# The end of a spectral mixer and MLP kernel: two-row sums, a last row tile in two pieces, and two half tiles moved

## The chip, the core and the metric

The kernel runs on one core of a Trainium2 chip. Its engines each follow an instruction stream of their own: PE multiplies matrices (PEld is its weight load), DVE, ACT and POOL work on vectors, SP issues transfers. The metric is the device time of one execution in microseconds (us), given as the median of several runs. A profile of one execution shows when every instruction ran; its span runs from the first instruction to the last.

## The reference

```
xn = layernorm(x)                       # x is 1 x 2048 x 512, float32
A  = irfft2( rfft2(xn) * (w_r + i w_i) )  # over rows and columns
h  = x @ w1 + b1  on xn:  h = xn @ w1 + b1          # w1 is 512 x 1792
B  = (h * tanh(softplus(h))) @ w2       # w2 is 1792 x 512
out = x + A + B
```

So one normalised input feeds a two-dimensional Fourier filter and a two-layer MLP with the Mish activation, and both results are added to the input.

## The kernel before

The 2048 rows are held as 16 row tiles of 128 rows, in four groups `g` of four tiles `s`. Numbers are split into two float16 halves, so a product is three passes on PE; the helper `mm3` (L68, L71, L72) issues the three.

The MLP is cut into 56 units (four groups times 14 blocks `f` of 128 hidden columns). `up(n)` makes a block of hidden values in PSUM tile `ph_g_f` (12 matmuls of 512 columns, L727); `mish` (L738, ACT), `a_hi` (L747, ACT) and `a_lo` (L750, DVE) turn it into `a_g_f`; `down(n)` multiplies it with w2 into four accumulators `pa_g_s` (12 matmuls, L68 to L72). `up` and `down` of a unit are each called a half tile. For the last row tiles of group 3, `mlp_rest` stops short of the last three blocks, and `end_of(s)` (L821 to L838) does those three for each row tile `s`, adds the result into the row tile (L837, DVE) and stores it. For `s` = 3 the columns are done in pieces with PSUM tiles `pe_0`, `pe_256`, and so on, after the rest of the accumulator was added at L816.

The Fourier branch is a stream of small units. Near its end, `dp_unit` fills PSUM tiles `psA`, which leave as `at` (L649 on ACT, L650 on DVE) and are turned through SP transfers into tiles `ai` (L656). `ip_pair` multiplies two `ai` tiles into a pair of PSUM tiles `psT` (L672); these leave as `tt` (L694 on ACT, L695 on DVE) and are stored to device memory as `d_t` (L700). When all of `d_t` is stored, it is loaded as 16 tiles `yi` (L857). The inverse along the rows makes `psY` from `yi`: for twelve of the row tiles in pairs (`s1_inverse_pair`, L108), for the four of group 0 one by one (`s1_inverse`). ACT copies `psY` into `ys` (L911, L912, or L878 for single rows), DVE makes sum and difference of a pair (L913, L914), and `add_rows` (L888 to L890) adds one row tile of `ys` into its row tile: 512 columns with the first half repeated, then 256 columns added and 256 subtracted. Row tiles of groups 0, 1 and 2 are called `m` and are stored at once (L778 for group 0, L782 otherwise); those of group 3 are called `y` and wait for the MLP.

Which half tiles stand between the steps of the Fourier stream is set by the table `HALVES`: one number for each step, saying how many half tiles are written ahead of it. From there a scheduler orders the instructions of each engine, with a few of them kept in program order; it may put a unit's matmuls inside another's. Every engine works its list strictly in order. Stores of `y` go half to SP's queue and half to ACT's. PSUM tiles tagged `f` (`psA`, `psT`, `psY`) share two buffers, and so do those tagged `h` (`ph`, `pe_0`).

Of the kernel before, what the change touches and what calls it, by code (L numbers as in the profile page):

```python
# [18 lines left out]
S, D, F = 2048, 512, 1792  # L19
P = 128  # L20
# [5 lines left out]
HALVES = (  # L26
# [4 lines left out]
)  # L31
NQ = 4
# [9 lines left out]
def spectral_mlp_kernel(ctx, tc, x, wt, w0, w1, b1, w2, cT, cIT, cM, out):  # L42
    nc = tc.nc
# [8 lines left out]
    ps_f = ctx.enter_context(tc.tile_pool(name="ps_f", bufs=2, space=PSUM))  # L52
    ps_h = ctx.enter_context(tc.tile_pool(name="ps_h", bufs=2, space=PSUM))
# [12 lines left out]
    def mm3(ps, stat, mov, start, stop, order=False):  # L66

        first = nc.tensor.matmul(ps, stat(0), mov(0), start=start, stop=False)  # L68
        if order:
            tc.keep_in_program_order(first)  # L70
        nc.tensor.matmul(ps, stat(0), mov(1), start=False, stop=False)  # L71
        nc.tensor.matmul(ps, stat(1), mov(0), start=False, stop=stop)  # L72
# [29 lines left out]
    def quarters(ps, stat, mov, order):  # L102

        for k, (hs, hm) in enumerate(PASSES):
            for r in range(2):
                for c in range(2):
                    rs, cs = slice(64 * r, 64 * r + 64), slice(64 * c, 64 * c + 64)
                    i = nc.tensor.matmul(ps(r, c)[cs], stat(r, c, hs)[rs], mov(r, c, hm)[rs], start=k == 0, stop=k == 2)  # L108
                    if order and (k, r, c) == (0, 0, 0):
                        tc.keep_in_program_order(i)  # L110
# [595 lines left out]
    macc, yacc = {}, {}  # L706
# [61 lines left out]
    def load_x(t, g, s, n):  # L768
        if g == 0:
            nc.sync.dma_start(t, xv[:, s : s + n, :])  # L770
            return
        for k in range(0, n, 2):
            for b in range(2):
                nc.sync.dma_start(t[64 * b : 64 * b + 64, k : k + 2, :], xw[:, 4 * g + s + k + b])

    def store_out(g, s, t, cs=slice(0, D)):
        if g == 0:
            nc.sync.dma_start(outv[:, s, cs], t)  # L778
            return
        for b in range(2):  # L780
            engine = nc.scalar if g == 3 and b else nc.sync
            engine.dma_start(outw[:, 4 * g + s // 2 * 2 + b, s % 2, cs], t[64 * b : 64 * b + 64])  # L782
# [13 lines left out]
    def mlp_rest(n_up, n_down, lag):  # L796

        while n_down < len(UP) - LAST:
            early = n_down % NFC == NFC - 1 and n_up - n_down == lag - 1
            if n_up < len(UP) and n_up - n_down < lag and not early:  # L800
                up(n_up)
                mish(n_up)
                a_hi(n_up)
                a_lo(n_up)
                if n_up % NFC == NFC - 1 and n_up // NFC < 3:
                    load_res(n_up // NFC)
                n_up += 1
                yield 1
            else:
                down(n_down)  # L810
                if n_down % NFC == NFC - 1:
                    mlp_end(n_down // NFC)
                n_down += 1
                yield 1
        r = yacc[3][3]
        nc.vector.scalar_tensor_tensor(r, pacc[3][3], sc["out"], r, op0=ALU.mult, op1=ALU.add)  # L816
        for s in range(4):
            end_of(s)
            yield 1

    def end_of(s):  # L821
        n = len(UP) - LAST
        g, pa, r = 3, pacc[3][s], yacc[3][s]
        for o, w in ((0, 256), (256, 128), (384, 128)) if s == 3 else ((0, D),):
            cs = slice(o, o + w)
            pool, tag = (ps_f, "f") if o == 384 else (ps_h, "h")
            ps = pool.tile([P, w], F32, tag=tag, name=f"pe_{o}") if s == 3 else pa
            for k in range(LAST):
                f = UP[n + k][1]
                mm3(  # L830
                    ps,
                    lambda i: act[n + k][:, i, s * P : (s + 1) * P],
                    lambda i: w2t[:, i, f, cs],
                    s == 3 and k == 0,
                    k == LAST - 1,
                )
            nc.vector.scalar_tensor_tensor(r[:, cs], ps, sc["out"], r[:, cs], op0=ALU.mult, op1=ALU.add)  # L837
            store_out(g, s, r[:, cs], cs)  # L838
# [24 lines left out]
    def s1_inverse(g, s):  # L863
        s2 = s
        yi = yis.pop(0)
        ps = ps_f.tile([P, 4, P], F32, tag="f", name=f"psY_{s2}")
        psr = ps.rearrange("p (b a) e -> p a b e", a=2)

        def slots(h, a):
            v = yi[:, :, h, :].rearrange("p (b a) e -> p a b e", a=2)[:, a]  # L870
            return v[:, :, ::-1] if a else v

        for a in range(2):
            mm3(psr[:, a], lambda h: sc["cIT"][:, s2, h, :], lambda h: slots(h, a), True, True, a == 0)
        if s % 2 == 0:
            ys[0] = tp.tile([P, 2, D], F32, tag="X", name=f"ys_{s2}", bufs=2)
        t = ys[0][:, s % 2]
        nc.scalar.activation(t, ps.rearrange("p a e -> p (a e)"), AF.Copy, scale=sc["k"])  # L878
        m = macc[g][:, s, :]
        add_rows(m, t)  # L880
        store_out(g, s, m)

    ys = {}

    def add_rows(m, t):
        mv = m.rearrange("p (b q) -> p b q", b=2)
        tv = t.rearrange("p (r q) -> p r q", r=2)
        nc.vector.tensor_add(mv, mv, tv[:, 0:1].to_broadcast((P, 2, 256)))  # L888
        nc.vector.tensor_add(mv[:, 0], mv[:, 0], tv[:, 1])
        nc.vector.tensor_sub(mv[:, 1], mv[:, 1], tv[:, 1])  # L890

    def s1_inverse_pair(g, s):
        s2, j = 4 * g + s, s // 2
        yi = [yis.pop(0) for _ in range(2)]
        ps = [ps_f.tile([P, 4, P], F32, tag="f", name=f"psY_{s2 + k}") for k in range(2)]
        psr = [t.rearrange("p (b a) e -> p a b e", a=2) for t in ps]

        def slots(k, h, a):
            v = yi[k][:, :, h, :].rearrange("p (b a) e -> p a b e", a=2)[:, a]
            return v[:, :, ::-1] if a else v  # L900

        for a in range(2):
            quarters(
                lambda r, c: psr[r][:, a],
                lambda r, c, h: sc["cIW"][:, s2 - 4 + c, h, :],
                lambda r, c, h: slots(c, h, a),
                a == 0,
            )
        t = tp.tile([P, 2, D], F32, tag="X", name=f"ys_{s2}", bufs=2)
        pe, po = (v.rearrange("p a e -> p (a e)") for v in ps)  # L910
        nc.scalar.activation(t[:, 0], pe, AF.Copy, scale=sc["k"])  # L911
        nc.scalar.activation(t[:, 1], po, AF.Copy, scale=sc["k"])  # L912
        nc.vector.tensor_add(t[:, 0], t[:, 0], t[:, 1])  # L913
        nc.vector.scalar_tensor_tensor(t[:, 1], t[:, 1], -2.0, t[:, 0], op0=ALU.mult, op1=ALU.add)  # L914
        if g not in macc:
            y = big.tile([P, 2, D], F32, tag="big", name=f"y_{s2}")
            load_x(y, g, s, 2)
        for h in range(2):
            m = macc[g][:, s + h, :] if g in macc else y[:, h, :]
            add_rows(m, t[:, h])  # L920
            if g in macc:
                store_out(g, s + h, m)
            else:
                yacc.setdefault(g, []).append(m)


    done = [0]
# [466 lines left out]
    for g, s, w in todo:  # L1394
        next(plan)
        (s1_inverse_pair if w == 2 else s1_inverse)(g, s)
# [136 lines left out]
```

## Time and profile before

| | us |
|---|---|
| median of 3 runs | 363.49 (363.40 to 363.56) |
| the profiled execution: its time | 363.37 |
| the profiled execution: its span | 361.6 |
| PE busy | 353.9 (98% of the span) |
| DVE busy | 278.5 (77%) |
| ACT busy | 187.7 (52%) |

The time holds about 1.8 us that the span does not. A row of the timeline reads: start, duration, engine, line, operation, output and inputs, shape, count. A duration on DVE or PE is longer than the distance to the next start, since each instruction's beginning overlaps the end of the one ahead. "SPq" and "ACTq" are the instructions of those engines that issue a transfer; the transfer itself lands later. "PEclk" or "granted clock" is the share of full speed at which PE ran; it is 0.998 over the whole span.

### The profile page before, as it was taken

To read this page: it belongs to the slowest core of one execution; us is meant where nothing else is said; L and a number is where in the kernel's file an instruction comes from. 1 tells how busy PE (TensorE), PEld (TensorE's weight loads), DVE (VectorE), ACT (ScalarE), POOL (GpSimd) and SP (SyncE) were. 2 spreads that over 40 slices of the span, in tenths; PEclk is the share of its full clock that TensorE was granted. 3 is DMA by queue.
4 is the path that set the end of the run, shared out by engine and by line. 5 is a ranking of instruction groups with operands and counts; after the bars stand their busy time and mean duration, and the time that the engine had idled before them with its cause. 6 is when DMAs were issued, how large, how long until landed. Compare 5 with 4: busy or idle time off the path is not lost.

```text
span 361.6 us, 6167 instructions
## 1 busy us (share of the span) xinstructions
PE 353.9 (98%) x2283; PEld 174.0 (48%) x2283; DVE 278.5 (77%) x543; ACT 187.7 (52%) x288; POOL 47.8 (13%) x49
## 2 busy tenths in 40 slices
PE   7999999999999999999999999999999999999994
PEld 2544444444444444545554445544554445444453
DVE  4898998886598776399998955996498933349995
ACT  5989974564654751525454365355443554445511
POOL 0020002303304500033030301130032000000000
PEclk9999999999999999999999999999999999999999
DMA  8945753699796657443611327218831524686566
GB/s 269 319 145 181 190 126 89 125 220 255 119 309 127 143 169 178 172 111 88 227 31 51 97 57 233 61 52 215 228 96 41 130 58 111 124 248 219 118 153 197
DMA packets 60702, 54.98 MB, mean 152 GB/s; under 512 B 16720, under 2 KB 49776, under 8 KB 60544
## 3 DMA queue, kind: packets, MB, share of 16 engines
q1 hardware_dynamic: 60192, 54.06, 56.6%
q10 hardware_dynamic: 480, 0.52, 0.5%
q8 instruction: 18, 0.29, 0.3%
q14 instruction: 12, 0.10, 0.1%
HBM read 34.61 MB, written 12.58 MB: 131 GB/s over the span
## 4 chain that ended last, share of the span: by engine, by line
PE 90%; DVE 6%; ACT 1%; DMA 1%; issue 0%; DVEq 0%
PE ph L727 39%; PE pa L68 13%; PE pa L71 12%; PE pa L72 12%; PE psT L672 2%; PE psS L108 1%; PE psY L108 1%; DMA x<-in_x_dram 1%; PE psA L68 1%; PE psA L71 1%; PE psA L72 1%; PE psP L516 1%; PE psP L526 1%; DVE u L425 1%; PE psP L519 1%; DVE xh L188 1%
## 5 line engine op out<-in xcount | busy, mean ns | idle before, releaser
L727 PE MATMUL ph<-xnT,w1t 128*128 128x512 f16 x672 | 153.4, 379 | 0.0
L727 PEld LDWEIGHTS <-w1t 128*128 128x128 f16 x672 | 64.6, 98 | 77.7 <-issue 2.7
L738 ACT ACTIVATE hb<-ph,b1t,fp_exp 128x512 f32<-128x512 f32 x56 | 43.2, 771 | 58.3 <-PE ph L727 58.2
L68 PE MATMUL pa<-w2t,a 128*128 128x512 f16 x181 | 68.7, 380 | 0.0
L71 PE MATMUL pa<-w2t,a 128*128 128x512 f16 x181 | 68.6, 379 | 0.0
L72 PE MATMUL pa<-w2t,a 128*128 128x512 f16 x181 | 68.6, 379 | 0.0
L750 DVE SCALAR_TENSOR_TENSOR a<-hb,ip_a,a 128x512 f16<-128x512 f32 x46 | 34.4, 749 | 34.4 <-ACT a L747 34.2
L747 ACT ACTIVATE a<-hb,ip_a 128x512 f16<-128x512 f32 x46 | 33.1, 720 | 2.3 <-DVE ip_a L288 1.2
L72 PEld LDWEIGHTS <-a 128*128 128x128 f16 x190 | 18.6, 98 | 21.0
L68 PEld LDWEIGHTS <-a 128*128 128x128 f16 x190 | 18.6, 98 | 20.8 <-issue 2.0
L71 PEld LDWEIGHTS <-a 128*128 128x128 f16 x190 | 18.6, 98 | 18.6
L249 POOL TENSOR_TENSOR xh<-xs,xh 128x512 f16<-128x512 f32 x12 | 15.4, 1292 | 56.7 <-ACT xh L223 23.4
L424 ACT ACTIVATE u<-w,sc_u 128x512 f16<-128x512 f32 x16 | 10.8, 713 | 22.1 <-DVE w L625 10.2
L531 DVE SCALAR_TENSOR_TENSOR z<-psP,z 128x512 f16<-128x512 f32 x16 | 10.8, 688 | 9.6 <-ACT z L530 9.6
L223 ACT ACTIVATE xh<-x,nb,rs 128x512 f16<-128x512 f32 x12 | 9.6, 806 | 13.1 <-DVE nb L217 11.7
L695 DVE SCALAR_TENSOR_TENSOR tt<-psT,tt 128x512 f16<-128x512 f32 x16 | 10.4, 683 | 7.3 <-ACT tt L694 7.3
L600 POOL TENSOR_TENSOR w<-X,wE 128x512 f32<-128x512 f32 x4 | 5.1, 1274 | 69.6 <-DVE X L593 69.6
L694 ACT ACTIVATE tt<-psT 128x512 f16<-128x512 f32 x16 | 8.8, 589 | 10.7 <-PE psT L672 8.8
L649 ACT ACTIVATE at<-psA 128x512 f16<-128x512 f32 x16 | 9.2, 589 | 9.4 <-PE psA L72 7.0
L156 DVE BATCH_NORM_STATS2 st<-x 128x6 f32<-128x512 f32 x16 | 10.3, 679 | 4.4 <-DMA x<-in_x_dram 4.4
L425 DVE SCALAR_TENSOR_TENSOR u<-w,sc_u,u 128x512 f16<-128x512 f32 x16 | 11.4, 747 | 2.4 <-ACT u L424 2.2
L530 ACT ACTIVATE z<-psP 128x512 f16<-128x512 f32 x16 | 9.4, 590 | 5.3 <-PE psP L526 5.2
(220 smaller groups left out, 576.7 us busy)
## 6 DMA issues: line engine op xcount, KB each, us to landing
d_y<-y SPq DMA_DIRECT2D x16, 256.0 KB, 4.2
wm<-in_wt_dram SPq DMA_DIRECT2D x8, 512.0 KB, 5.2
ai<-at SPq DMA_DIRECT2D x64, 64.0 KB, 2.2
d_t<-tt SPq DMA_DIRECT2D x32, 128.0 KB, 2.5
w1s<-in_w_dram SPq DMA_DIRECT2D x7, 512.0 KB, 9.0
w2s<-in_w_dram SPq DMA_DIRECT2D x7, 512.0 KB, 3.4
x<-in_x_dram SPq DMA_DIRECT2D x12, 256.0 KB, 7.4
yt<-d_y SPq DMA_DIRECT2D x6, 512.0 KB, 4.1
```

Of the source, the lines that this page charges most:

```text
L68: first = nc.tensor.matmul(ps, stat(0), mov(0), start=start, stop=False)
L71: nc.tensor.matmul(ps, stat(0), mov(1), start=False, stop=False)
L72: nc.tensor.matmul(ps, stat(1), mov(0), start=False, stop=stop)
L249: engine.tensor_sub(self.xh[s][:, 1, :], self.xs[s], self.xh[s][:, 0, :])
L424: nc.scalar.activation(dst_h, src, AF.Copy, scale=scale)
L425: nc.vector.scalar_tensor_tensor(dst_l, src, scale, dst_h, op0=ALU.mult, op1=ALU.subtract)
L531: nc.vector.scalar_tensor_tensor(zl, psv, 2.0**-14, zh, op0=ALU.mult, op1=ALU.subtract)
L695: nc.vector.scalar_tensor_tensor(tt[:, :, 1, :], ps[r], 2.0**-12, tt[:, :, 0, :], op0=ALU.mult, op1=ALU.subtract)
L727: nc.tensor.matmul(ph[n + k], w1t[:, hw, dc, f * P : (f + 1) * P], xnT[g][:, hx, dc, :], start=(hw, hx, dc) == (0, 0, 0), stop=(hw, hx, dc ...
L738: nc.scalar.activation(hbt[n], ph.pop(n), AF.Mish, bias=b1t[:, f : f + 1], scale=s_exp[part_of(f)])
L747: nc.scalar.activation(act[n][:, 0, :], hbt[n], AF.Copy, scale=sc["a"])
L750: nc.vector.scalar_tensor_tensor(act[n][:, 1, :], hbt.pop(n), sc["a"], act[n][:, 0, :], op0=ALU.mult, op1=ALU.subtract)
```

## The change

There are three edits. In `add_rows` the row index becomes a dimension of the operands, so that `s1_inverse_pair` calls it once for both row tiles of a pair instead of once for each; the stores follow both sums. In `end_of` the last row tile's columns are done as 0 to 255 and 256 to 511 instead of 256, 128 and 128, and the second piece takes a PSUM buffer of tag `f`. In `HALVES` the numbers of the last steps differ: among the steps that hold the last `ip_pair`s half tiles come one or two steps later, and among the six inverse pairs one comes two steps earlier.

```diff
 HALVES = (
...
-    1, 0, 1, 0, 2, 0, 2, 0, 1, 1, 1, 0, 0, 0, 1, 0, 2, 0, 0, 1, 1, 0, 1, 0, 0, 1, 3, 1, 1, 1, 1, 2,
+    1, 0, 1, 0, 2, 0, 2, 0, 1, 1, 1, 0, 0, 0, 1, 0, 2, 0, 0, 1, 0, 1, 0, 0, 1, 0, 4, 1, 1, 2, 1, 1,
...
     def end_of(s):
...
-        for o, w in ((0, 256), (256, 128), (384, 128)) if s == 3 else ((0, D),):
+        for o, w in ((0, 256), (256, 256)) if s == 3 else ((0, D),):
             cs = slice(o, o + w)
-            pool, tag = (ps_f, "f") if o == 384 else (ps_h, "h")
+            pool, tag = (ps_f, "f") if o == 256 else (ps_h, "h")
...
     def add_rows(m, t):
-        mv = m.rearrange("p (b q) -> p b q", b=2)
-        tv = t.rearrange("p (r q) -> p r q", r=2)
-        nc.vector.tensor_add(mv, mv, tv[:, 0:1].to_broadcast((P, 2, 256)))
-        nc.vector.tensor_add(mv[:, 0], mv[:, 0], tv[:, 1])
-        nc.vector.tensor_sub(mv[:, 1], mv[:, 1], tv[:, 1])
+        n = m.shape[1]
+        mv = m.rearrange("p h (b q) -> p h b q", b=2)
+        tv = t.rearrange("p h (r q) -> p h r q", r=2)
+        nc.vector.tensor_add(mv, mv, tv[:, :, 0:1].to_broadcast((P, n, 2, 256)))
+        nc.vector.tensor_add(mv[:, :, 0], mv[:, :, 0], tv[:, :, 1])
+        nc.vector.tensor_sub(mv[:, :, 1], mv[:, :, 1], tv[:, :, 1])
...
+        m = macc[g][:, s : s + 2, :] if g in macc else y
+        add_rows(m, t)
         for h in range(2):
-            m = macc[g][:, s + h, :] if g in macc else y[:, h, :]
-            add_rows(m, t[:, h])
             if g in macc:
-                store_out(g, s + h, m)
+                store_out(g, s + h, m[:, h, :])
             else:
-                yacc.setdefault(g, []).append(m)
+                yacc.setdefault(g, []).append(m[:, h, :])
```

DVE's list at the very end of the program, before. `m` is the last row tile of group 0, `pa` the accumulator of row tile 2, `pe` the pieces of row tile 3:

```order
L888 TENSOR_TENSOR m_0_986<-m_0_986,ys_2_4079 128x512
L837 SCALAR_TENSOR_TENSOR y_14_3747<-pe_0_4109,s_out_580,y_14_3747 128x256
L889 TENSOR_TENSOR m_0_986<-m_0_986,ys_2_4079 128x256
L890 TENSOR_TENSOR m_0_986<-m_0_986,ys_2_4079 128x256
L837 SCALAR_TENSOR_TENSOR y_14_3747<-pe_256_4122,s_out_580,y_14_3747 128x128
L837 SCALAR_TENSOR_TENSOR y_14_3747<-pe_384_4135,s_out_580,y_14_3747 128x128
L1529 UNCONDITIONAL_BRANCH
```

The same list in the change (lines behind 884 have moved by one):

```order
L889 TENSOR_TENSOR m_0_986<-m_0_986,ys_2_4061 128x512
L837 SCALAR_TENSOR_TENSOR y_14_3744<-pe_0_4091,s_out_580,y_14_3744 128x256
L890 TENSOR_TENSOR m_0_986<-m_0_986,ys_2_4061 128x256
L891 TENSOR_TENSOR m_0_986<-m_0_986,ys_2_4061 128x256
L837 SCALAR_TENSOR_TENSOR y_14_3744<-pe_256_4104,s_out_580,y_14_3744 128x256
L1530 UNCONDITIONAL_BRANCH
```

The order is the same, and two additions of 128 columns became one of 256.

SP's list at the end, as the difference of the two. The numbers of `y` differ only because tiles were numbered anew:

```order
-L782 DMA out_dram<-y_3747 64x512
-L782 DMA out_dram<-y_3747 64x256
+L782 DMA out_dram<-y_3744 64x512
+L782 DMA out_dram<-y_3744 64x256
 L778 DMA out_dram<-m_986 128x512
-L782 DMA out_dram<-y_3747 64x128 x2
-L1529 UNCONDITIONAL_BRANCH
+L782 DMA out_dram<-y_3744 64x256
+L1530 UNCONDITIONAL_BRANCH
```

Behind the store of `m` stands one store of 64 rows by 256 columns where two of 64 by 128 stood.

PE's list around the last `ip_pair`, in the change. Ahead of these rows stand nine of the twelve matmuls of `ph_3_8`, and the names in brackets are the counters that a row waits for; those called DMAHW count transfers that landed:

```order
L727 LDWEIGHTS w1t_89
L727 MATMUL ph_3_8_3564<-xnT_3_1169,w1t_89 128x512
L672 LDWEIGHTS cMt_87 [waits DMAHW1_49,DMAHW0_49]
L672 MATMUL psT_15_3541<-ai_15_3481,cMt_87 64x512 [waits DVE_49]
L672 LDWEIGHTS cMt_87 [waits DMAHW7_49,DMAHW6_49]
L672 MATMUL psT_14_3540<-ai_15_3481,cMt_87 64x512 [waits DVE_49]
```

Before, all twelve matmuls of `ph_3_8` stood ahead of `psT_15`; now three of them stand behind the pair, and a `down` that stood ahead of the first pair (`psT_12`, `psT_13`) stands behind it.

More of the change, by code (lines that the diff above doesn't have):

```diff
@@ L878, in s1_inverse @@
         nc.scalar.activation(t, ps.rearrange("p a e -> p (a e)"), AF.Copy, scale=sc["k"])
-        m = macc[g][:, s, :]
-        add_rows(m, t)
-        store_out(g, s, m)
+        m = macc[g][:, s : s + 1, :]
+        add_rows(m, ys[0][:, s % 2 : s % 2 + 1])
+        store_out(g, s, m[:, 0, :])
     ys = {}
     def add_rows(m, t):
-        mv = m.rearrange("p (b q) -> p b q", b=2)
-        tv = t.rearrange("p (r q) -> p r q", r=2)
-        nc.vector.tensor_add(mv, mv, tv[:, 0:1].to_broadcast((P, 2, 256)))
-        nc.vector.tensor_add(mv[:, 0], mv[:, 0], tv[:, 1])
-        nc.vector.tensor_sub(mv[:, 1], mv[:, 1], tv[:, 1])
+        n = m.shape[1]
[4 more added lines that the diff above has]
+        nc.vector.tensor_sub(mv[:, :, 1], mv[:, :, 1], tv[:, :, 1])
     def s1_inverse_pair(g, s):
```

## The prediction

> **What bounds the kernel now.** I read the page first, then the busy time by stretches of the end, then the chain that ended last, then the single instructions and stores of the last 8 us.
>
> ```profile
> span 361.6 us, 6167 instructions
> 302.90:320.30 17.40, 17.40 (x101) 7.32 (x99) 4.74 (x7) 6.60 (x10) 0.00 (x0) 1.00 0.55 130
> 320.30:344.00 23.70, 23.70 (x231) 11.47 (x231) 21.47 (x44) 13.13 (x20) 0.00 (x0) 1.00 0.66 192
> 344.00:354.80 10.80, 10.80 (x65) 6.09 (x63) 10.66 (x22) 2.07 (x3) 0.00 (x0) 1.00 0.67 177
> 354.80:357.00 2.20, 2.02 (x28) 1.76 (x25) 1.87 (x5) 0.69 (x1) 0.00 (x0) 1.00 0.92 264
> ```
>
> The stretch rows give length, then busy time of PE, PEld, DVE, ACT and POOL. From 302.90, where the first moved instruction stands, to 354.80, PE is busy for all of every stretch. DVE is nearly as full (21.47 of 23.70, 10.66 of 10.80), but a full engine is no bound while PE never waits for it. So nothing that only relieves DVE there can shorten the time, and PE's amount of work does not change: nine matmuls of 256 columns cost what eighteen of 128 do. What can move the time lies behind PE's last work.
>
> ```profile
> 354.56 0.27 PE L72 MATMUL psY<-yi_w,cITt 128*128 128x256 f16 x1
> 356.61 0.22 PE L72 MATMUL pe<-w2t,a 128*128 128x128 f16 x1
> 354.87 0.70 ACT ys L878
> 355.59 0.69 DVE m L888
> 355.59 0.69 DVE L888 TENSOR_TENSOR m<-m,ys 128x512 f32<-128x512 f32 x1 [0.33 <-ACT ys L878]
> 356.20 0.48 DVE L837 SCALAR_TENSOR_TENSOR y<-pe,s_out,y 128x256 f32<-128x256 f32 x1
> 357.26 0.60 DVE L837 SCALAR_TENSOR_TENSOR y<-pe,s_out,y 128x128 f32<-128x128 f32 x2
> ```
>
> The first two rows are the last matmul of the last `psY` and PE's last of all, which ends at 356.83. The chain goes from that `psY` over ACT (354.87) to DVE's sum of the last `m` (355.59), and DVE then runs without a stop to 357.26 + 0.60 = 357.86. DVE stood idle for 0.33 us ahead of that sum: whatever it was late with before, it has caught up there. This 0.33 us is the cover under which the pair sums lie. Behind DVE come the stores:
>
> ```profile
> 357.38 0.43 SPq L778 DMA_DIRECT2D out_dram<-m  x1
> 357.90 0.47 SPq L782 DMA_DIRECT2D out_dram<-y  x1
> 358.46 0.58 SPq L782 DMA_DIRECT2D out_dram<-y  x1
> 358.21 0.55 ACTq L782 DMA_DIRECT2D out_dram<-y  x1
> SPq L1529 <- DMA out_dram<-y: 1.5, 1, 1.5
> out_dram<-m SPq DMA_DIRECT2D x4, 256.0 KB, 2.8
> out_dram<-y SPq DMA_DIRECT2D x2, 32.0 KB, 2.3
> ```
>
> SP issues its last store from 358.46 to 359.04 and then waits 1.5 us for the landing, to 360.54; the span ends 1.04 us later with the closing of the program, which the change leaves alone. ACT's last store begins 0.25 us ahead of SP's. So the last thing that sets the end is SP's third store in a row: `m`, piece, piece.
>
> **The change part by part.**
>
> *Last row tile in two pieces.* DVE: the second piece now takes 0.48 us (the 256-column row) instead of 0.60 for two, so `y` is whole at 357.74 instead of 357.86. PE had the data at 356.83, so PE is not in the way. SP, though, is issuing `m` until 357.38 + 0.43 = 357.81, and its next issue began at 357.90 although its piece was ready by then; the 0.12 us that DVE gains is hidden by that issue and costs or earns nothing. What counts is that the one store from 357.90 is now the last, where one from 358.46 was: 0.56 us less of queue. Against this the store carries 64 KB instead of 32. No row of 64 KB has its landing shown. Its nearest rows are 32 KB with 2.3 us and 256 KB with 2.8 us from issue to landing; the last one today took 360.54 - 358.46 = 2.08. So it lands at 357.90 + 2.08 = 359.98 at the earliest and 357.90 + 2.8 = 360.70 at the latest, a gain of 0.56 down to a loss of 0.16. I take 2.3, the nearer row by size: 360.20, a gain of 0.34. ACT's only second piece can start at 357.77 and lands ahead of that by the same 2.3.
>
> *Pair sums.* Rows of one pair before:
>
> ```profile
> 336.74 1.28 DVE L888 TENSOR_TENSOR m<-m,ys 128x512 f32<-128x512 f32 x2
> 337.94 0.42 DVE L889 TENSOR_TENSOR m<-m,ys 128x256 f32<-128x256 f32 x1
> 339.28 0.74 DVE L750 SCALAR_TENSOR_TENSOR a<-hb,ip_a,a 128x512 f16<-128x512 f32 x1
> L888 DVE TENSOR_TENSOR m<-m,ys 128x512 f32<-128x512 f32 x12 | 7.9, 684 | 0.3 <-ACT ys L878 0.3
> L443 DVE TENSOR_REDUCE mxw<-wm 128x1 f32<-128x1024 f32 x8 | 9.5, 1210 | 0.0
> L572 DVE TENSOR_TENSOR r<-g,c0t 4x256 f32<-4x256 f32 x4 | 4.6, 1148 | 0.0
> ```
>
> From start to start, two of 512 columns take 1.20 us (0.60 each) and four of 256 take 1.34 (0.335 each), 2.54 together. So an instruction has a fixed part of 2 x 0.335 - 0.60 = 0.07 us, and the three that fall away in a pair save about 0.21: 2.33 us. The bounds: a saving of nothing, and, by durations instead of distances, 2 x 0.684 less the 1.210 that L443 takes for 1024 columns, plus 4 x 0.42 less 2 x 0.684: 0.47. For six pairs this is 1.3 us of DVE time (0 to 2.8). It shortens nothing: PE does not wait for DVE, and the last row's sum waits for ACT, which waits for PE. If that cover were gone, a pair that cost more than 2.54 us would first use up the 0.33 us of idle time and then delay the last `m`, the pieces and their stores. The first row of a pair is now stored with the second, about 0.67 - 0.21 = 0.46 us later than before; all those stores stand far ahead of the last ones in SP's queue.
>
> *Moved half tiles.* PE does the same work in another order, so only a new wait can cost. The inverse pair `psY_6` comes one `up` later and DVE gets it later; DVE's lateness can only shrink by this. The other place is `psT_14`, `psT_15`:
>
> ```profile
> 302.90 0.38 PE L68 MATMUL pa<-w2t,a 128*128 128x512 f16 x1
> 305.58 0.84 PE L672 MATMUL psT<-ai,cMt 64*64 64x512 f16 x12
> 306.36 2.76 PE L727 MATMUL ph<-xnT,w1t 128*128 128x512 f16 x12
> 309.05 0.84 PE L672 MATMUL psT<-ai,cMt 64*64 64x512 f16 x12
> 317.77 2.59 PE ph L727 x12
> 306.17 0.60 SPq L656 DMA_DIRECT2D ai<-at  x1
> DMA to landing us min/median/max: 2.1/2.2/2.7
> ```
>
> Before, a `down` ran from 302.90, the first pair of `psT` at 305.58, `ph_3_8` at 306.36, the second pair at 309.05. Now the first pair runs at about 303.00 and the `down` behind it, so `ph_3_8` still begins at 306.36. Twelve such matmuls step in 2.59 us (last of the PE rows), 0.216 each, and the 2.69 from 306.36 to 309.05 hold a changeover of 0.10. Nine of them are done at 308.30, so the second pair is due at 308.40. It needs `ai_15`, whose last transfer is issued at 306.17 and lands 2.2 us later (2.1 to 2.7): 308.37, between 308.27 and 308.87. So the spare time, 0.68 us before, is down to 0.03. Bounds: no wait, or 0.47 us on PE; I take 0.05. Queued behind that wait is PE itself, the three matmuls of `ph_3_8`, all later half tiles and so the end: it is paid in full. The stores of `tt` and the loads of `yi` that follow begin earlier than before, because the pair and ACT's copies come ahead of the hidden block's; `psY` cannot be late through them.
>
> *Sum.* -0.34 + 0.05 = -0.29 us: span 361.3, and 363.37 - 0.29 = 363.08 for the profiled execution. The median of the runs is 0.12 above that execution, so 363.20.
>
> **The rivals.**
>
> *The landing wait eats the gain.* `ai_15` lands at the slow end of its range, PE stands for 0.3 to 0.47 us, and the time is 363.4 to 363.7, say 363.6. For it: the spare time of 0.03 us. Against it: the median landing.
>
> *The longer store hides the gain.* SP's store waits behind the 256 KB of `m`, or a 64 KB store needs 2.65 us and more; then it lands when today's does: 363.5. For it: the 2.8 us row, and a DMA share of 0.92 in the last stretch of PE. Against it: the 32 KB stores stand behind the same `m` today and took 2.1 to 2.3.
>
> *All of the queue's gain.* The store lands as fast as today's last (2.08) and PE does not wait: 363.49 - 0.56 = 362.9.
>
> *Two-row sums are slow, and the kernel is slower.* DVE could take more than one step a column for operands with one more dimension. For it: the row of L572, a 256-column operation with a repeated operand, took 1148 ns where 420 is usual. Against it: L888 repeats its operand too, at the common 684 ns. At 1.3 times the rate, a pair takes 3.03 us, 0.49 more than now; three to six pairs pass on 1.5 to 2.9 us, less the 0.33 of idle time, so DVE ends 1.1 to 2.6 us late: 364.3 to 365.8, say 365.0. It decides from 2.60 us a pair on, if all six pass it on.
>
> *Stores that run one after another.* If the second piece's store only began once the first had landed, dropping it would save 2.3 us: 361.2. Against it: with 2.3 us each from 357.90, the second would land at 362.5, behind the end of the span. The Trainium skill, page "DMA: Bandwidth & Descriptors", section "Rules for kernel authors", says that many small transfers should become one large one, as below 64 KB they are mostly overhead. Its section "Anatomy of one DMA — SWDGE (gpsimd) path" gives about 2.0 us fixed plus bytes / 436e9: an estimate by it is a saving of about 2.0 us if nothing overlaps, 361.5. The trace disagrees: the second store was issued 0.56 us behind the first and landed 2.08 us after its own issue, so the fixed parts overlap and only the 0.56 can be saved.
>
> **How the numbers follow.** Forecast, 363.0 to 363.4: 0.60, likeliest 363.2. Landing wait 0.13, hidden gain 0.12, full gain 0.07, slow sums 0.06, stores in turn 0.02. The range must leave out 2 in 10 at most: from 362.8, just below the full gain, to 363.7, the upper end of the landing wait. A difference of 0.2% is 0.73 us, about what can be told from no change here. Forecast, wait, hidden gain and full gain lie within it, less 0.06 for their tails: 0.86. Faster holds the stores in turn and 0.05 of tails beyond the full gain, 0.07; slower the slow sums and 0.01 of an unlucky landing, 0.07.
>
> **What would show it.** Right: DVE's last addition ends near 357.74 plus PE's shift, SP issues two stores behind the last `pe_0` piece instead of three, and the wait for the last landing ends some 0.3 us earlier; a pair's three sums take about 2.33 us and DVE's idle time ahead of the last `m` grows past 0.33; PE stands still for less than 0.1 us ahead of the second `psT` pair. Wrong: a gap there of 0.3 us or more, a sum of 1024 columns far over 1.3 us, or a last store that needs 2.6 us to land. The forecast fails altogether if PE is found waiting anywhere behind 309 us.

## The result and the profile after

The changed kernel takes 364.24 us, the median of 15 runs (363.71 to 364.89), where the kernel before took 363.49 in the same comparison (15 runs, 363.26 to 363.90). The ratio is 1.0021, with a 95% interval of 1.0015 to 1.0028: slower by 0.15 to 0.28%, where 363.2 and no change were forecast, and above the upper end of the range, 363.7. The profiled execution took 364.2 and has a span of 362.3, 0.7 more than before.

To compare two executions, times "from the start" below are counted from the first matmul of `ph_3_7`, which begins the same stretch in every kernel (300.31 before, 300.22 after).

The page of the kernel after, its waits on PE, its stretches, PE's timeline around the last `psT` pair and the first `psY`, and SP's issue of the last two transfers of `ai_15`:

```profile
span 362.3 us, 6122 instructions
```

```profile
PE psT L672 <- DMA ai<-at: 0.2, 1, 0.2
```

```profile
302.90:320.30 17.40, 17.23 (x97) 7.58 (x96) 4.85 (x7) 6.66 (x10) 0.00 (x0) 1.00 0.61 149
```

```profile
306.27 2.11 PE L727 MATMUL ph<-xnT,w1t 128*128 128x512 f16 x9
308.55 0.96 PE L672 MATMUL psT<-ai,cMt 64*64 64x512 f16 x12 [0.17 <-DMA ai<-at]
309.45 0.82 PE L727 MATMUL ph<-xnT,w1t 128*128 128x512 f16 x3
...
320.56 0.85 PE L108 MATMUL psY<-yi_z,cITt 64*64 64x256 f16 x24
```

```profile
305.57 1.25 SPq L656 DMA_DIRECT2D ai<-at  x2
```

PE is no longer busy for the whole of the stretch from 302.90: 17.23 of 17.40. It waits for the transfers of `ai`, as one rival said, and the bracket names them. The nine matmuls begin at 306.27, and by the prediction's own count (9 x 0.216 + 0.10 = 2.04) the pair was due at 308.31. It begins at 308.55, 0.24 late. From its start to the next block's it takes 0.90 where the row of 309.05 before took 0.77 (to 309.82). Together 0.37. That is what arrives at `psY_12`: 320.56 - 300.22 = 20.34 from the start, against 320.29 - 300.31 = 19.98 before.

The trace also holds the counters that a transfer raises as it lands, and they explain both parts. The last transfer of `ai_15` is issued at 306.21 and has landed at 308.42, 2.21 us later. The pair's first matmul begins 0.13 us behind that landing. The first matmul of the pair's other tile begins at 308.68, another 0.13 behind, although its own transfers had landed by 307.11: it stands behind the first in PE's list. In the kernel before, where the last transfer had landed 0.69 us ahead of the pair, the first four matmuls begin within 0.01 us of each other (309.05 to 309.06).

DVE's timeline for the first pair of `psY`, after and then before:

```profile
323.39 0.69 DVE L914 TENSOR_TENSOR ys<-ys 128x512 f32<-128x512 f32 x1 [0.40 <-ACT ys L913]
324.12 0.69 DVE L915 SCALAR_TENSOR_TENSOR ys<-ys 128x512 f32<-128x512 f32 x1
324.84 1.22 DVE L889 TENSOR_TENSOR y<-y,ys 128x1024 f32<-128x1024 f32 x1
326.10 0.69 DVE L890 TENSOR_TENSOR y<-y,ys 128x512 f32<-128x512 f32 x1
326.71 0.69 DVE L891 TENSOR_TENSOR y<-y,ys 128x512 f32<-128x512 f32 x1
327.31 0.68 DVE L914 TENSOR_TENSOR ys<-ys 128x512 f32<-128x512 f32 x1
```

```profile
323.11 0.69 DVE L913 TENSOR_TENSOR ys<-ys 128x512 f32<-128x512 f32 x1 [0.40 <-ACT ys L912]
323.84 0.69 DVE L914 SCALAR_TENSOR_TENSOR ys<-ys 128x512 f32<-128x512 f32 x1
324.45 1.28 DVE L888 TENSOR_TENSOR y<-y,ys 128x512 f32<-128x512 f32 x2
...
326.99 0.69 DVE L913 TENSOR_TENSOR ys<-ys 128x512 f32<-128x512 f32 x1
```

A pair with its sums takes 327.31 - 323.39 = 3.92 us after and 326.99 - 323.11 = 3.88 before. Three instructions fewer save nothing. The rows show why. An instruction that reads what the one ahead of it wrote starts when that one has ended (324.12 to 324.84, 0.72, and 324.84 to 326.10, 1.26). One that does not starts 0.60 behind the other (326.71 to 327.31). Before, the first row's sum did not read what L914 wrote, so only 0.61 lay between them; the sum over both rows needs both.

SP's timeline at the end, its waits, and the issues by size, after:

```profile
348.99 2.39 SPq L782 DMA_DIRECT2D out_dram<-m  x4
351.48 0.53 SPq L778 DMA_DIRECT2D out_dram<-m  x1
...
353.10 1.25 SPq L778 DMA_DIRECT2D out_dram<-m  x1
...
357.65 0.43 SPq L778 DMA_DIRECT2D out_dram<-m  x1
358.17 0.47 SPq L782 DMA_DIRECT2D out_dram<-y  x1
```

```profile
SPq L1530 <- DMA out_dram<-y: 2.0, 2, 1.8
```

```profile
out_dram<-m SPq DMA_DIRECT2D x4, 256.0 KB, 3.7
out_dram<-y SPq DMA_DIRECT2D x2, 64.0 KB, 3.3
```

and SP's timeline before for the same stores:

```profile
347.80 2.38 SPq L782 DMA_DIRECT2D out_dram<-m  x4
350.52 0.36 SPq L778 DMA_DIRECT2D out_dram<-m  x1
...
352.58 0.36 SPq L778 DMA_DIRECT2D out_dram<-m  x1
```

The first row is the four stores of the last pair of `m`. They begin 48.77 us from the start, where they began at 47.49 before. Of these 1.28 us 0.37 are PE's wait; for the rest, the first two stores now wait for the sums of both rows. The last store is issued at 358.17, ahead of the 358.46 of before, but it needs 3.3 us and lands at 361.47, where before the last landing was at 360.54.

The difference adds up from the start: DVE's last addition ends at 358.02 - 300.22 = 57.80 (before 57.86 from a start at 0.31, 57.55), +0.25; the last store lands 3.45 behind DVE's end instead of 2.68, +0.77; the closing of the program takes 0.83 instead of 1.06, -0.23. The sum is +0.79; `ph_3_7` itself begins 0.09 earlier, and 0.70 is left. So two things made the kernel slower, a wait on PE and a late landing at the end.

### The profile page after: what moved, and what is told of

Its sections match the earlier page's. It is cut to its first block, busy times and chain, and to the rows that moved or that the text cites. A ratio compares the mean times of both kernels' runs of the same rounds, so it can differ in the third digit from the quotient of the medians.

```text
span 362.3 us, 6122 instructions
## 1 busy us (share of the span) xinstructions
PE 353.7 (98%) x2274; PEld 173.9 (48%) x2274; DVE 278.5 (77%) x524; ACT 187.8 (52%) x288; POOL 47.8 (13%) x49
## 4 chain that ended last, share of the span: by engine, by line
PE 78%; DVE 14%; ACT 2%; DMA 2%; SPq 1%; issue 1%; DVEq 0%
PE ph L727 35%; PE pa L68 11%; PE pa L71 10%; PE pa L72 10%; DVE m L889 2%; PE psT L672 2%; SPq L656 1%; PE psS L108 1%; DVE ys L915 1%; DVE ys L914 1%; DVE m L891 1%; DMA x<-in_x_dram 1%; PE psP L516 1%; DVE a L750 1%; PE psA L72 1%
## 5 line engine op out<-in xcount | busy, mean ns | idle before, releaser
L72 PEld LDWEIGHTS <-a 128*128 128x128 f16 x187 | 18.3, 98 | 21.1
L68 PEld LDWEIGHTS <-a 128*128 128x128 f16 x187 | 18.3, 98 | 20.8 <-issue 2.0
L71 PEld LDWEIGHTS <-a 128*128 128x128 f16 x187 | 18.3, 98 | 18.6
```

## The experiments

All ratios are to the kernel before, measured beside each. "Moves", "pieces" and "sums" name the three edits.

**The three edits one at a time.**

The moves alone:

```diff
-    ..., 2, 0, 0, 1, 1, 0, 1, 0, 0, 1, 3, 1, 1, 1, 1, 2,
+    ..., 2, 0, 0, 1, 0, 1, 0, 0, 1, 0, 4, 1, 1, 2, 1, 1,
```

> Only the table of half tiles of the change; sums and pieces as before. Theory 'landing wait plus stores': PE waits for ai_15 ahead of the second psT pair, as in the changed kernel (0.37 us of PE time later from there on), and all of it reaches the end: +0.35 us (+0.25 to +0.5) against the kernel before. Rival 'longer last store': the same +0.35, since both have the wait. Rival 'later inverse pair': the whole loss of 0.75 us is in the table, as DVE gets psY_6 later: +0.75.

Measured: 364.14 against 363.66, ratio 1.0016 (1.0007 to 1.0025). PE's timeline with the moves alone:

```profile
306.31 2.11 PE L727 MATMUL ph<-xnT,w1t 128*128 128x512 f16 x9
308.91 0.96 PE L672 MATMUL psT<-ai,cMt 64*64 64x512 f16 x12 [0.49 <-DMA ai<-at]
...
320.92 0.85 PE L108 MATMUL psY<-yi_z,cITt 64*64 64x256 f16 x24
```

The last transfer of `ai_15` is issued at 306.60 here and lands at 308.77. The pair is 308.91 - 306.31 - 2.04 = 0.56 late, and with its 0.13 more length 0.69. `psY_12` comes at 320.92 - 300.25 = 20.67 from the start, 0.69 later than before. So the whole loss of this edit is at that one place.

The pieces alone:

```diff
-        for o, w in ((0, 256), (256, 128), (384, 128)) if s == 3 else ((0, D),):
+        for o, w in ((0, 256), (256, 256)) if s == 3 else ((0, D),):
...
-            pool, tag = (ps_f, "f") if o == 384 else (ps_h, "h")
+            pool, tag = (ps_f, "f") if o == 256 else (ps_h, "h")
```

> Only the last row tile in two pieces of 256 columns. Theory 'landing wait plus stores': this edit alone does what was forecast, one store issue less in SP's queue: -0.3 us (-0.5 to -0.1). Rival 'longer last store': a 64 KB store at the end lands some 0.7 us later than one of 32 KB: +0.2 to +0.4. Rival 'later inverse pair': -0.3.

Measured: 363.36 against 363.66, ratio 0.9994 (0.9985 to 1.0003). The sign is as forecast, but the interval holds no change. The issues by size:

```profile
out_dram<-y SPq DMA_DIRECT2D x2, 64.0 KB, 2.5
```

SP issues its last store at 358.17. A 64 KB store takes 2.5 us here and lands at 360.67. In this execution PE and DVE run 0.28 later than before (`ph_3_7` begins 0.08 later, and `psY_12` takes 0.2 longer; see the last section), so against DVE the last store is issued 0.29 + 0.28 = 0.57 earlier than before, as forecast, and of that 0.42 goes to its longer landing (2.5 against 2.08). The same store, issued at the same 358.17, needs 3.3 us in the kernel after: what is slow there is not its size.

The sums alone:

```diff
+        m = macc[g][:, s : s + 2, :] if g in macc else y
+        add_rows(m, t)
         for h in range(2):
-            m = macc[g][:, s + h, :] if g in macc else y[:, h, :]
-            add_rows(m, t[:, h])
             if g in macc:
-                store_out(g, s + h, m)
+                store_out(g, s + h, m[:, h, :])
```

> Only the sums over both rows of a pair at once. Theory 'landing wait plus stores': the sums save DVE nothing (a pair takes 0.04 us more, because each of the three now waits for the one ahead of it) and hold back the stores of a pair's first row, so the transfers are bunched into the last microseconds: +0.5 us (+0.3 to +0.8), with PE's end where it was. Rivals 'longer last store' and 'later inverse pair': no change, 0 +- 0.1.

Measured: 364.15 against 363.66, ratio 1.0013 (1.0004 to 1.0022). SP's timeline with the sums alone:

```profile
348.69 2.39 SPq L782 DMA_DIRECT2D out_dram<-m  x4
351.18 0.53 SPq L778 DMA_DIRECT2D out_dram<-m  x1
...
352.81 1.81 SPq L778 DMA_DIRECT2D out_dram<-m  x1
...
358.18 1.36 SPq L782 DMA_DIRECT2D out_dram<-y  x2
```

```profile
SPq L782 <- DMA out_dram<-y: 0.4, 1, 0.4
```

The first row of group 0 is whole at 350.72 (the last sum, DVE 350.30 + 0.42), but SP is still issuing the pair's stores and takes it at 351.18. The next `m` holds SP for 1.81 us, where it took 0.36 before. At the end SP waits 0.4 us for an earlier store of `y` to land, and only then issues the last one, at 359.07 where it was 358.46 before. The span of this profile is 0.7 us longer than before, and not all of that is the stores': DVE ends at 358.14, 0.28 later than before, because `psY_12` takes 0.29 longer in this execution, which kernels without these sums do too (last section). From DVE's end to the end of the span it takes 362.3 - 358.14 = 4.2 us, and 361.6 - 357.86 = 3.7 before. That part is the stores'.

Three edits by themselves give +0.16 + 0.13 - 0.06 = +0.23%, and together +0.21%. With 0.09% either way on each of the three, that agrees with edits that add.

**Which part of the table.** The edit's first part, around the last `psT`, alone, and then its second part, among the inverse pairs, alone:

```diff
+    ..., 2, 0, 0, 1, 0, 1, 0, 0, 1, 0, 4, 1, 1, 1, 1, 2,
```

> Only the first part of the table: the half tiles among the last two ip_pairs, as in the change; the table among the inverse pairs, sums and pieces as before. The table as a whole cost 0.16% (0.6 us). Theory 'landing wait': the whole cost is PE's wait for ai_15 ahead of psT_15, which stands in this part: +0.4 to +0.6 us, and a PE wait on ai in the profile. Rival 'later inverse pair': +0.0 to +0.1, as the DVE lateness of the other part was the cost.

```diff
+    ..., 2, 0, 0, 1, 1, 0, 1, 0, 0, 1, 3, 1, 1, 2, 1, 1,
```

> Only the second part of the table: one half tile two steps earlier among the inverse pairs. Theory 'landing wait': no change (0 +- 0.1 us), as PE does not wait there and DVE has caught up by the last row. Rival 'later inverse pair': +0.4 to +0.6 us, the cost of the whole table.

Measured: the first part 364.14 against 363.50, ratio 1.0016 (1.0007 to 1.0024); the second 363.49 against 363.50, ratio 0.9997 (0.9988 to 1.0005). PE's timeline with the first part alone, then with the second part alone:

```profile
306.36 2.10 PE L727 MATMUL ph<-xnT,w1t 128*128 128x512 f16 x9
308.62 0.96 PE L672 MATMUL psT<-ai,cMt 64*64 64x512 f16 x12 [0.16 <-DMA ai<-at]
```

```profile
309.01 0.96 PE L672 MATMUL psT<-ai,cMt 64*64 64x512 f16 x12
```

308.62 - 306.36 - 2.04 = 0.22 late, and 0.13 for the longer pair. The cost of the moves is the first part, where PE meets the transfers of `ai_15`; the later inverse pair is free within the interval. The second part alone leaves all twelve matmuls ahead of the pair, and yet the pair runs long there: SP issued the last transfer at 306.68 in that execution, 0.6 us later from the start than in the profile of before, it landed at 308.87, and of the 0.68 us to spare only 0.14 were left, too little for the other tile's matmul. The time of that issue moves from one profile to the next.

**What the sums cost: three suspects.** DVE is later, by 3.92 - 3.88 a pair; the pair's first row is released later; and four stores are issued in one go when the next rows are due. The first run has late stores without the two-row sums: the sums of single rows as before, second row first, and the stores behind both.

```diff
+        for h in (1, 0):
+            add_rows(ms[h], t[:, h])
         for h in range(2):
...
+                store_out(g, s + h, ms[h])
```

> Kernel before with single-row sums, but the second row of a pair first, so that the stores of both rows wait for the end of the pair; DVE has the same instructions. It separates two ways in which the sums may cost: if the time at which a pair's stores are released is the cause, +0.3 us (+0.2 to +0.6); if DVE's own time for a pair is the cause, no change (0 +- 0.1).

Measured: 363.59 against 363.66, ratio 1.0000 (0.9991 to 1.0009). Against what was expected there is no loss. But the edit delayed too little: the first of the four stores is issued at 348.36, 47.83 from the start, against 47.49 before and 48.39 with the sums. It speaks against any delay being costly, and not against a delay of 0.9 us. SP was held here too, for 1.51 us by a store of `y` issued at 353.47, so that such a hold alone isn't the cost. The stores of a pair in the turned order:

```diff
+        if g in macc:
+            for h in (1, 0):
+                store_out(g, s + h, ms[h])
```

> Kernel before, its DVE list unchanged, but SP is given the second row's stores of a pair ahead of the first row's, so that both wait for the end of the pair, as with the two-row sums (there the last pair's first store is issued 0.11 us behind the start of the addition that follows the pair; in the kernel before 0.55 us ahead of it, in the late-stores run 0.22 ahead). Theory 'stores held back': SP's queue is then late for the last rows as with the two-row sums: +0.3 us (+0.15 to +0.5). Rival 'DVE time': no change (0 +- 0.1), since the two-row sums cost by the 0.04 us a pair that DVE takes more.

Measured: 363.45 against 363.50, ratio 0.9998 (0.9989 to 1.0007). Here the first store is issued at 347.79, as early as before, so that it tests nothing of the delay.

DVE's lateness by itself: one copy of 128 x 1 more in each pair, for which the computation has no use.

```diff
             add_rows(m, t[:, h])
+            if h:
+                nc.vector.tensor_copy(sp.tile([P, 1], F32, tag="tax", name=f"tax_{s2}", bufs=2), t[:, 1, 0:1])
```

> Kernel before with one operation of a single column more on DVE behind each of the six pairs (about 0.07 us from start to start, 0.4 us in all); all stores as before, four a pair, the first row's early. The two-row sums made DVE 0.24 us late in all. Rival 'DVE time': such lateness is what costs, so +0.4 to +0.6 us here. Theories 'SP's queue' and 'bytes late': at most +0.2 us, as the stores of a pair's first row still leave 0.5 us ahead of its end and DVE catches up by the last row.

Measured: 363.70 against 363.59, ratio 0.9996 (0.9987 to 1.0005). DVE's `y` sum of L816 comes at 48.48 from the start, against 48.04 before and 48.28 with the sums alone. DVE is later than with the sums, and nothing is lost: the cover of the prediction, DVE's idle time ahead of the last `m`, holds.

The number of stores: the two-row sums as in the change, with both rows of a pair leaving in two stores of 64 x 2 x 512 instead of four of 64 x 512. Then the same stores with the sums of before.

```diff
+    def store_pair(g, s):
+        for b in range(2):
+            nc.sync.dma_start(outw[:, 4 * g + s + b], macc[g][64 * b : 64 * b + 64, s : s + 2, :])
...
-                store_out(g, s + h, m[:, h, :])
+            store_pair(g, s)
```

> Two-row sums as in the change (table and pieces as before), but the two rows of a pair in groups 1 and 2 leave with two stores of 64 rows by 2 x 512 instead of four of 64 by 512: same bytes, same time of release, half of SP's issues. The two-row sums alone cost +0.13%. Theory 'SP's queue' (four issues of 0.6 us begin only at the pair's end, and the stores of the last rows queue behind them): the cost falls to +0.0 to +0.2 us. Rivals 'DVE time' (0.04 us a pair more) and 'bytes late' (transfers bunched): it stays at +0.3 to +0.6 us.

> Sums, table and pieces as before; only the two rows of a pair in groups 1 and 2 leave with two stores instead of four, so the first row's bytes wait for the end of the pair. This is the late release that the run with the stores' order turned round did not bring about (its first store went out as early as before). Rival 'bytes late': +0.2 to +0.5 us. Theories 'SP's queue' and 'DVE time': no loss, -0.2 to +0.1 us.

Measured: 363.56 against 363.59 in both, ratios 0.9997 (0.9988 to 1.0005) with the two-row sums and 0.9996 (0.9988 to 1.0005) without. SP's timeline and issues with two-row sums and merged stores:

```profile
348.70 1.25 SPq L786 DMA_DIRECT2D out_dram<-m  x2
350.76 0.36 SPq L778 DMA_DIRECT2D out_dram<-m  x1
...
352.81 0.36 SPq L778 DMA_DIRECT2D out_dram<-m  x1
```

```profile
out_dram<-m SPq DMA_DIRECT2D x6, 256.0 KB, 2.9
```

The stores are released at the same time as with the sums alone (348.70 and 348.69), DVE is as late (L816 at 48.29 and 48.28 from the start), and the bytes are the same. Only the issues are half as many, 1.25 us instead of 2.39, and the cost is gone. The two ratios, 1.0013 and 0.9997, differ by 0.0016, with a half width of about 0.0012 if the two intervals are independent.

The profiles show the same without the lateness of PE, if the end of the span is counted from DVE's last end. With three pieces it takes 4.2 us with the sums alone and 3.7 in each of the nine other kernels, the two-row sums with merged stores among them (361.6 - 357.86). With two pieces it takes 4.3 in the kernel after and 3.4 to 3.5 in the three others. So it is late in the two kernels that have two-row sums and four stores a pair, and in no other.

The bytes that the transfer engines move fit this. The stretches of the end before, with the sums alone, with the sums and merged stores, and after; the last column is GB/s:

```profile
348.00:350.00 2.00, 2.00 (x14) 1.23 (x13) 1.97 (x5) 0.32 (x1) 0.00 (x0) 1.00 0.48 112
350.00:356.00 6.00, 6.00 (x45) 3.88 (x44) 5.60 (x12) 1.74 (x3) 0.00 (x0) 1.00 0.87 250
```

```profile
348.00:350.00 2.00, 2.00 (x14) 1.20 (x13) 1.97 (x5) 0.09 (x2) 0.00 (x0) 1.00 0.09 22
350.00:356.00 6.00, 6.00 (x41) 3.75 (x40) 5.55 (x12) 2.02 (x3) 0.00 (x0) 1.00 0.85 232
360.00:362.00 2.00, 0.00 (x0) 0.00 (x0) 0.00 (x0) 0.00 (x0) 0.00 (x0) 0.65 0.15 40
```

```profile
348.00:350.00 2.00, 2.00 (x14) 1.23 (x13) 1.97 (x5) 0.33 (x1) 0.00 (x0) 1.00 0.02 6
350.00:356.00 6.00, 6.00 (x45) 3.88 (x43) 5.84 (x12) 1.74 (x3) 0.00 (x0) 1.00 0.91 268
```

```profile
348.00:350.00 2.00, 2.00 (x14) 1.20 (x13) 2.00 (x4) 0.09 (x2) 0.00 (x0) 1.00 0.02 5
350.00:356.00 6.00, 6.00 (x40) 3.76 (x39) 5.82 (x13) 2.02 (x3) 0.00 (x0) 1.00 0.84 210
360.00:362.00 2.00, 0.00 (x0) 0.00 (x0) 0.00 (x0) 0.00 (x0) 0.00 (x0) 0.50 0.28 94
```

Before, 0.22 MB moved between 348 and 350 (112 GB/s for 2 us). With the two-row sums that stretch is nearly empty, and the bytes come behind it. With merged stores they are made up for at once: 1.61 MB from 350 to 356, against 1.50 before. With four stores only 1.39 go in that time, in the kernel after 1.26, and some (0.08 and 0.19 MB) is still moving behind 360. A later PE isn't the reason: the pieces alone, with DVE's last `m` as late as in these two (355.87), moved 108 and 249 GB/s in the two stretches, as much as before. The tail behind 360 is a weaker sign, since a late PE makes one too (53 GB/s with the moves alone). The median landing of the 256 KB stores is 3.7 us with the sums alone and in the kernel after, 2.8 before, 2.9 merged.

The Trainium skill, page "DMA: Bandwidth & Descriptors", section "Issuing engines are not separate DMA queues", says that the time to issue a transfer is usually small beside the transfer itself. Here one issue took 0.6 us and such a store of 128 KB lands in 2.3 to 2.4, so that four in a row held SP for as long as one takes to land (2.39), and halving the issues was worth the whole of the cost. Whether it is the issuing itself or some other property of having more and smaller stores in the queue was not separated.

**Towards a better kernel.** The pieces, with the second store of `tt_14` and `tt_15` each on ACT's queue; and then the same with merged stores for the pairs, sums and table as before.

```diff
-                nc.sync.dma_start(
+                engine = nc.scalar if fgs[0] == 14 and u else nc.sync
+                engine.dma_start(
                     d_t[r, f : f + 4].rearrange("f c q e -> (c q) f e"),
```

> Two pieces, table and sums as before, and the second stores of tt_14 and tt_15 issued from ACT's queue instead of SP's. In three of four profiles with the table of before, PE stood 0.16 to 0.28 us within psY_12, whose yi tiles land in the same 0.2 us in which it begins. Theory 'margin at psY_12': with four instead of six waits in SP's queue the loads of yi begin about 1.2 us earlier, the wait is gone, and the time is 0.2 to 0.5 us below the kernel before (363.1 to 363.4). Rival 'pieces alone': the same as the two pieces alone, -0.06% (-0.2 us).

```diff
+        if g in macc:
+            store_pair(g, s)
```

> Two pieces, the second stores of tt_14 and tt_15 on ACT's queue (363.07 us and 0.08% below the kernel before in its run), and one store of two rows instead of two in groups 1 and 2. Theory 'SP's queue': no worse than without the merged stores, 362.9 to 363.2 (-0.3 to -0.6 us). Rival 'bytes late': the late release costs 0.2 to 0.5, 363.3 to 363.6.

Measured: 363.07 against 363.50, ratio 0.9992 (0.9983 to 1.0001), and with merged stores 363.20 against 363.59, ratio 0.9986 (0.9977 to 0.9994). The second is the one kernel here whose interval lies below one: it is faster by 0.14%, less than the 0.2% that was called the least that can be told. That the merged stores add to the first isn't shown, since the two intervals overlap. Nor is it shown by the runs that the second queue adds to the pieces alone (0.9992 and 0.9994), although `psY_12` runs without a stop in both of these profiles.

## Why the prediction was wrong

*What bounds the kernel* held. PE is full behind 310 us, DVE's lateness alone costs nothing (the copy in each pair, ratio 0.9996), and what moved the time was a wait on PE and the stores behind it.

*Moved half tiles* had the right mechanism and the wrong size. The step that failed is the term "I take 0.05" with "no wait, or 0.47 us on PE" as its bounds: it measured 0.37 in the kernel after, 0.35 with the first part of the table alone and 0.69 with the moves alone; by medians these two lost 0.64 and 0.48 us. The landing time was right: the last `ai` transfer took 2.18 to 2.21 us in all fourteen profiles. Two other things were left out. The time of its issue was taken as fixed. It was 5.86 us from the start in the profile of before (306.17 - 300.31) and 5.99 in the kernel after (306.21 - 300.22), and over the fourteen profiles it goes from 5.75 to 6.42; with the moves alone it was 6.35, and there the wait is 0.3 us longer. And PE was to begin at the landing, where its first matmul came 0.13 us behind it and the other tile's 0.13 behind that. In the kernel after this is 0.13 + 0.01 + 0.26, less the 0.03 to spare: 0.37. With 0.03 us to spare the wait should have been the likeliest case and not a rival at 0.13. By itself it doesn't leave the range: 363.20 with 0.37 in place of 0.05 is 363.52.

*Pair sums* failed at two steps. The first is the price: "the three that fall away in a pair save about 0.21" took the fixed part from instructions that do not read one another's result. The two-row sums take 327.31 - 324.84 = 2.47 us, not 2.33, and the wait of 0.11 that the first row's sum used to cover falls on top. The row that would have shown it stood in the trace of before: L913 to L914 takes 0.73 there and L914 to L888 0.61. By itself this cost nothing. The second step is the one that cost, and that took the time out of the range: "all those stores stand far ahead of the last ones in SP's queue", with which a later release was put at nothing. A later release was named, of 0.46 us; with the sums alone it is 0.90 (48.39 from the start, 47.49 before). But the queue was looked at for places only, not for time: four issues of 0.6 us each, released later, stand ahead of stores that come every 2 us, and what they push back is not made up by the end. In the sum for the kernel after, the last store was to land 360.20 - 357.74 = 2.46 us behind DVE's end and landed 3.45 behind it: 0.99, the largest miss. The rival of "two-row sums are slow" asked about DVE's rate alone (the rate was usual, 1.22 us for 1024 columns), and no rival asked about the stores.

*Last row tile in two pieces* held as far as can be told. The store takes 2.5 us (forecast 2.3, between 2.08 and 2.8) where it stands without the late stores; 0.1 to 0.2 us less of closing came on top, which had been called unchanged. By medians it is -0.30 us against -0.34 forecast; the ratio's interval, times 363.66, reaches from -0.55 to +0.11. In the kernel after the same store lands in 3.3 us, and the gain is lost: by 356 us fewer bytes have been moved there than with the pieces alone, and that they are what the store lands behind is argued from this, not measured.

*"`psY` cannot be late through them"* was right: the loads of `yi` begin at 315.41 after and 316.61 before, and `psY_12` runs without a stop. The load that it needs last lands 1.58 us ahead of it (318.98), where before it was 0.14 (last section).

*The rivals.* The landing wait was the right one of the five, and even at its 363.6 it stood alone. The slow landing came too, not by the store's size; it goes with the late stores ahead of it. Neither stores in turn nor a slow rate of DVE showed. The rival of two-row sums was right about the sign by luck: it named DVE's rate. The estimate of 2.0 us beside the stores in turn is from a section of the Trainium skill on transfers that GpSimd issues (page "DMA: Bandwidth & Descriptors", section "Anatomy of one DMA — SWDGE (gpsimd) path"); the stores here are issued by SP and ACT.

*DVE's idle time* ahead of the last `m` was to grow past 0.33. It shrank to nothing: the chain of the kernel after, whose copy on ACT waits for DVE's own sum.

```profile
354.80 0.35 DVE m L891
...
355.15 0.70 ACT ys L878
...
355.87 0.69 DVE m L889
```

The 0.33 us of cover were used up, and no more than that: with the pieces alone, where PE is as late and DVE is not, ACT's copy also begins at 355.15.

The chances had 0.86 on a change within 0.2% and 0.07 on slower. The single edits are each within 0.2% (0.16, 0.13 and 0.06), and it is two of them on one side that came out beyond it; the cases of the prediction let only one thing go wrong at a time.

## What to carry to other kernels

Where a store is released later, count the issues that stand in its queue from there to the end, each with its duration, and not only its place; a few larger stores can give back what a later release takes. Before instructions are merged to save their fixed part, look at whether the merged one must wait for a result that the first of the single ones did not need. Where the work that waits for a transfer is moved ahead, compare the time to spare with how much the transfer's issue moves between executions (0.67 us here) and with what lies between landing and first use (0.13 to 0.26 us), and not with the landing time alone.

## What was not expected

An instruction on DVE that reads the output of the one ahead starts 0.72 us behind it at 512 columns, where one that does not starts 0.60 or 0.61 behind (rows above): 0.11 us for each such step.

`psY_12` has a margin that the profile of before did not show. In five kernels whose edits all lie behind it (the pieces and the sums alone, the two orders of stores, merged stores with the sums of before), it took 1.00 to 1.14 us instead of 0.85 in the profiled execution, and 0.92 with the copy on DVE. The timeline of PE with the sums alone:

```profile
320.27 1.14 PE L108 MATMUL psY<-yi_z,cITt 64*64 64x256 f16 x24
```

PE waits there for the second load of `yi_z`. Its counter shows it landed at 320.52, and the second matmul of `psY_12` begins at 320.57; in all six kernels that matmul begins 0.04 to 0.05 us behind this landing. In the profile of before the load landed at 320.15, 0.14 us ahead of `psY_12`, and with merged stores and `tt` stored by two queues at 319.99, 0.60 ahead. Such a wait can make two single profiles of like kernels differ by 0.3 us, and for that reason the verdicts above rest on all runs and not on one profile.
